# Separate weight tiles for Q, K and V, and two moves of gate/up blocks in a fused layer-norm, sliding-window attention and gated-MLP kernel

## The chip, the cores and the metric

The kernel runs on one core of one Trainium2 chip. The metric is device time in microseconds (us), lower is better. TensorE (PE in the profile) does the matrix products, VectorE (DVE) and ScalarE (ACT) read the sums and do elementwise work, GpSimd (POOL) masks, and SyncE (SP) issues nearly all DMA transfers.

## The reference

```python
def reference(A_x, A_wqkv, A_wo, B_x, B_w_gate, B_w_up, B_w_down):   # S=2048, D=640, F=1536
    x = A_x
    xn = _layernorm(x, axis=-1)
    return x + _A_ref(xn, A_wqkv, A_wo) + _B_ref(xn, B_w_gate, B_w_up, B_w_down)

# _A_ref: H = 32 heads of 20, window of 256 positions
    q, k, v = (x @ wqkv) split into three and into heads
    scores = einsum("bhqd,bhkd->bhqk", q, k) * (Dh ** -0.5)
    mask = (idx[:, None] - idx[None, :] >= 0) & (idx[:, None] - idx[None, :] < W)
    p = softmax(where(mask, scores, -1e9))
    return einsum("bhqk,bhkd->bhqd", p, v) joined over heads @ wo

# _B_ref
    h = sigmoid(x @ w_gate) * (x @ w_up)
    return h @ w_down
```

All arrays are bf16. Attention and the gated MLP read the same normalised x; their results and x are added.

## The kernel before

The 2048 positions are worked in four chunks of 512. For each chunk the kernel normalises x, turns it (`xnT`, by DMA transposes for chunks 1 to 3), and then has three kinds of TensorE work beside attention itself. **Q/K blocks** (`proj_block`): ten a chunk, Q0 to Q4 and K0 to K4, each of five matmuls of 512 columns. The sums are copied to a staging tile `st` (VectorE for Q, ScalarE for K), stored to a DRAM scratch (`sq`, `sk`), and read back spread over partitions as `qT` and `kT` by `spread`. The pool of `st` has six buffers. **V blocks** (`g_v`): eight a chunk. **GLU blocks** (`g_gu`): twelve a chunk; each has five matmuls for the gate, a tanh on ScalarE, five matmuls for up, and one VectorE instruction that writes `h`. An **output stage** (`g_out`) adds, for the four rows of 128 positions of a chunk, `h` times `w_down` (`down`) and the attention result times `wo` (`add_wo`); its arguments `between` and `ahead` take GLU blocks that are worked between the first row's two kinds of sums, or ahead of them.

Attention of a chunk is a series of score steps (16 for chunk 0, 20 for the others, numbered through as t = 0 to 75). A step's scores (L490) go to one PSUM tile `ps`, of which there is one buffer; ScalarE takes the exponential (L496), GpSimd masks, and after the last step of a head group `pv` (L523) multiplies by V.

The order on every engine is the order of the program. Attention's steps are the skeleton; a planner (`Fill`) pulls the other work in between, in the order of the `fill.add` calls, each with a cost in nanoseconds for TensorE. A step pulls at least about 1800 ns of it, and more where work is left over. `fill.until("qk1")` at the start of chunk 1 takes all that is left of an entry. Entries of cost 0 only issue DMAs: x of the next chunk (`load_x`), `wo` turned in DRAM (`turn_wo`, eight transfers into `wo_i`), `w_down` (`load_wd`, five), and the zero pads of the second scratch (`clear_next`, two). In the list of before they stand between chunk 0's last GLU block and `qk1`. The helper `mix` alternates two generators. All of these transfers, the `st` stores, `load_wo` and the `spread` loads go through SyncE's queue in the order of the program:

```python
    fill.add("gu0b", mix(g_gu(0, 4, 12), norms1, 0), 8 * GU)
    fill.add("x2", later(load_x, 2), 0)
    fill.add("wo_i", later(turn_wo), 0)
    fill.add("wd", later(load_wd), 0)
    fill.add("pads", later(clear_next), 0)
    fill.add("qk1", g_qk(1), 50 * MM)
    fill.add("v1", mix(g_v(1), g_gu(1, 0, 2), 1, 2), 40 * 136 + 2 * GU)
```

The Q, K and V weights lie side by side in one SBUF tile `wqkv`. It is loaded by four transfers (V in two halves, Q, K). A Q/K block reads its weights with a stride of five elements.

Of the kernel before, what the change touches and what calls it, by code (L numbers as in the profile page):

```python
# [9 lines left out]
P = 128  # L10
S = 2048
D = 640
# [3 lines left out]
DC = D // P  # L16
# [9 lines left out]
HALF = 320  # L26
# [11 lines left out]
BF16 = mybir.dt.bfloat16  # L38
# [55 lines left out]
def kernel(  # L94
# [11 lines left out]
    nc = tc.nc  # L106
# [4 lines left out]
    def pool(name, bufs, **kw):  # L111
        return ctx.enter_context(tc.tile_pool(name=name, bufs=bufs, **kw))

    const = pool("const", 1)
# [22 lines left out]
    def load_x(c):  # L137
        t = xp.tile([P, SBC, D], BF16, name="xc")
        xc[c] = t
        nc.sync.dma_start(out=t, in_=xr[:, c * SBC:(c + 1) * SBC, :])  # L140

    wqkv = const.tile([P, DC, 3 * D], BF16, name="wqkv")
    wqkv_r = A_wqkv.rearrange("(c p) n -> p c n", p=P)
    wg = [const.tile([P, DC, FS], BF16, name=f"wg{k}") for k in range(F // FS)]
    wu = [const.tile([P, DC, FS], BF16, name=f"wu{k}") for k in range(F // FS)]
# [2 lines left out]

    ones = nc.const_aps.tensor(1.0, [P, CW], BF16)
    def load_wqkv(part):  # L150
        nc.sync.dma_start(out=wqkv[:, :, part * D:(part + 1) * D],
                          in_=wqkv_r[:, :, part * D:(part + 1) * D])

    xc[0] = xp.tile([P, SBC, D], BF16, name="xc")

# [1 line left out]
        queue.dma_start(out=xc[0][:, s, :], in_=xr[:, s, :])  # L157

    def load_v(hf):
        a = 2 * D + hf * HALF  # L160
        nc.sync.dma_start(out=wqkv[:, :, a:a + HALF], in_=wqkv_r[:, :, a:a + HALF])

    load_rows(0, nc.sync)
    load_rows(1, nc.sync)
    load_rows(3, nc.sync)
    load_v(0)
    load_rows(2, nc.sync)
    load_v(1)
# [12 lines left out]
    def load_gu(t, w, k, lo=0, hi=FS):  # L181
        nc.sync.dma_start(out=t[k][:, :, lo:hi],
                          in_=w.rearrange("(c p) f -> p c f", p=P)[:, :, k * FS + lo:k * FS + hi])
# [32 lines left out]
    def load_wo():  # L216
        for i in range(HG):
            nc.sync.dma_start(out=wo[32 * i:32 * i + 32, :, :],
                              in_=wo_i[i].rearrange("(m j) n -> j m n", j=32))
# [63 lines left out]
    def turn_block(c, s):  # L283
        nc.sync.dma_start(out=xnT[c][:, :, s * P:(s + 1) * P], in_=xns.pop((c, s)), transpose=True)
# [5 lines left out]
    qk = {}  # L290
    vt = {}

    def proj_block(w, c, m):


        base = 0 if w == "q" else D
        ps = ps_d.tile([P, CW], FP32, name="pqk", tag="d")
        for d in range(DC):
            wt = wqkv[:, d, base:base + D].rearrange("p (k m) -> p m k", m=DC)
            nc.tensor.matmul(ps, lhsT=wt[:, m, :], rhs=xnT[c][:, d, :],  # L300
                             start=(d == 0), stop=(d == DC - 1))
        st = stp.tile([P, CW], BF16, name="st")
        if w == "q":
            nc.vector.tensor_copy(out=st, in_=ps)
        else:
            nc.scalar.copy(out=st, in_=ps)
        dst = scratch[w, c % 2].rearrange("(h j) s -> h j s", j=32)
        nc.sync.dma_start(out=dst[:, 4 * m:4 * m + 4, :], in_=st)

    def spread(w, c, g0, g1):  # L310

        half, first = divmod(g0, GH)
        if first == 0:
            qk[w, c, half] = (qp if w == "q" else kp).tile([P, GH, CW], BF16, name=w + "T")
        src = scratch[w, c % 2].rearrange("(a b p) s -> b p a s", a=2, p=P)
        for b in range(g0 // 2, g1 // 2):
            o = 2 * b - half * GH
            nc.sync.dma_start(out=qk[w, c, half][:, o:o + 2, :], in_=src[b])

    def new_v(c, s):  # L320
        v = vp.tile([P, 2, VH], BF16, name="v")
        vt[c * SBC + s] = v
        nc.gpsimd.memset(v[:, :, 0:16 * VW].rearrange("p k (h d) -> p k h d", d=VW)[:, :, :, DH:VW], 0.5)
        nc.gpsimd.memset(v[:, :, 16 * VW:], 0.0)

    def project_v(c, s, hf, home=ps_d, tag="d"):
        ps = home.tile([P, CW], FP32, name="pv", tag=tag)
        for d in range(DC):
            nc.tensor.matmul(ps[:, 0:HALF], lhsT=xnT[c][:, d, s * P:(s + 1) * P],  # L329
                             rhs=wqkv[:, d, 2 * D + hf * HALF:2 * D + (hf + 1) * HALF],  # L330
                             start=(d == 0), stop=(d == DC - 1))
        return ps

# [7 lines left out]
    def proj_v(c, s, hf, copy):  # L341
        copy_v(c, s, hf, project_v(c, s, hf), copy)
# [21 lines left out]
    def g_turns(c):  # L364
        for s in range(SBC):
            turn_block(c, s)
            yield 0

    def g_qk(c):
        for w in "qk":  # L370
            for m in range(DC):
                proj_block(w, c, m)
                if c == 0 and w == "q" and m == 1:
                    load_x(1)
                if c == 0 and w == "q" and m == 3:
                    load_gu(wu, B_w_up, 0, FS // 2)
                if c == 1 and w == "q" and m == 3:
                    load_wo()
                if c and w == "k" and m == 1:
                    spread("q", c, 0, GH)  # L380
                yield 5 * MM
        if c == 0:
            spread("q", c, 0, 2)
            spread("k", c, 0, 2)
            spread("q", c, 2, 4)
            spread("k", c, 2, 4)

    def g_v(c):
        for s in range(SBC):
            new_v(c, s)  # L390
            for hf in range(2):
                proj_v(c, s, hf, nc.scalar.copy if hf else nc.vector.tensor_copy)
                if hf == 0:
                    yield 5 * 136
            if s == 0:
                spread("k", c, 0, 2)
                spread("k", c, 2, GH)
            if s == 1:
                spread("q", c, GH, NG)
                spread("k", c, GH, NG)  # L400
            yield 5 * 136
# [4 lines left out]
    def part(w, d, f):  # L406
        k, first = divmod(f * P, FS)
        return w[k][:, d, first:first + P]

    def g_gu(c, f0, f1):  # L410
        for f in range(f0, f1):
            pg = ps_d.tile([P, CW], FP32, name="pg", tag="d")
            for d in range(DC):
                nc.tensor.matmul(pg, lhsT=part(wg, d, f), rhs=xnT[c][:, d, :],  # L414
                                 start=(d == 0), stop=(d == DC - 1))
            th = tp.tile([P, CW], FP32, name="th")
            nc.scalar.activation(out=th, in_=pg, func=TANH, scale=0.5)  # L417
            yield 5 * MM
            pu = ps_d.tile([P, CW], FP32, name="pu", tag="d")
            for d in range(DC):  # L420
                nc.tensor.matmul(pu, lhsT=part(wu, d, f), rhs=xnT[c][:, d, :],  # L421
                                 start=(d == 0), stop=(d == DC - 1))
            h = hp.tile([P, CW], BF16, name="h")
            ht[c, f] = h
            nc.vector.scalar_tensor_tensor(out=h, in0=th, scalar=1.0, in1=pu, op0=ADD, op1=MULT)  # L425
            yield 5 * MM
# [39 lines left out]
    def g_out(c, between, ahead=()):  # L466
        nxt = new_rows(c, 0)
        for s in range(SBC):
            rows = nxt
            if s == 0:  # L470
                yield from ahead
            if s + 1 < SBC:
                nxt = new_rows(c, s + 1)
            ys = [ps_d.tile([P, CW], FP32, name=f"y{i}", tag="d") for i in range(2)]
            for y, cut in zip(ys, HALVES):
                yield from down(c, s, y, cut)
            if s == 0:
                yield from between
            outp(c, s, ys, rows)
            yield 10 * 136  # L480
# [117 lines left out]
    def mix(a, b, first, every=1, rest=True):  # L598

        for k, cost in enumerate(a):  # L600
            yield cost
            if k >= first and (k - first) % every == 0:
                yield next(b, 0)
        if rest:
            yield from b
# [74 lines left out]
    fill = Fill()  # L680
    GU = 10 * MM
    OUT = 4 * 34 * 136
    APART = 1800
    FIRST_PART = 1000
    def later(load, *args):
        load(*args)
        yield 0

    norms1 = g_norms(1, True)
    norms2 = g_norms(2, True)  # L690
    norms3 = g_norms(3, False)
    fill.add("gu0a", mix(g_gu(0, 0, 4), norms1, 4, 1, False), 4 * GU)
    fill.add("gu0b", mix(g_gu(0, 4, 12), norms1, 0), 8 * GU)
    fill.add("x2", later(load_x, 2), 0)
    fill.add("wo_i", later(turn_wo), 0)
    fill.add("wd", later(load_wd), 0)
    fill.add("pads", later(clear_next), 0)
    fill.add("qk1", g_qk(1), 50 * MM)
    fill.add("v1", mix(g_v(1), g_gu(1, 0, 2), 1, 2), 40 * 136 + 2 * GU)
    fill.add("out0", mix(g_out(0, g_gu(1, 2, 3)), norms2, 1, 1), OUT + GU)  # L700
    fill.add("x3", later(load_x, 3), 0)
    fill.add("qk2", g_qk(2), 50 * MM)
    fill.add("v2", mix(g_v(2), g_gu(1, 3, 7), 0, 1), 40 * 136 + 4 * GU)
    fill.add("gu1b", mix(g_gu(1, 7, 12), norms3, 0, 1, False), 5 * GU)
    fill.add("out1", mix(g_out(1, g_gu(2, 0, 1)), itertools.chain(norms3, g_turns(3)), 1, 3), OUT + GU)
    fill.add("qk3", g_qk(3), 50 * MM)
    fill.add("v3", mix(g_v(3), g_gu(2, 1, 5), 0, 1), 40 * 136 + 4 * GU)
    fill.add("gu2", g_gu(2, 5, 12), 7 * GU)
# [101 lines left out]
```

## Time and profile before

| what | us |
|---|---|
| time, median of 3 runs (lowest to highest) | 309.93 (309.67 to 310.23) |
| the profiled execution's own time | 309.64 |
| its span, first to last instruction | 307.9 |
| TensorE busy | 300.4 |
| ScalarE busy | 198.4 |
| VectorE busy | 171.2 |
| GpSimd busy | 168.7 |
| granted TensorE clock | 1.00 throughout |

The span is what the views divide; the 1.74 us between it and the execution's own time lie outside the first and last instruction. Times in the views count from the span's start. In a timeline line the columns are start, duration, engine, line of the kernel, operation, tile written and tiles read, shape and count; a bracket at the end tells how long the engine was idle before and what ended that. A waits line tells who waited for whom, the total in us, how often, and the longest. `PEld` is TensorE's weight load, `SPq` the issue of a DMA by SyncE, `ACTq` an instruction of ScalarE's sequencer. The ends of matmuls are modelled and overlap the next start.

### The profile page before, as it was taken

Reading aid. Unit: us, or ns where it says so; the run is one execution under the profiler, and the core shown is the slowest. Engines: PE = TensorE matmul, PEld = TensorE weight load, DVE = VectorE, ACT = ScalarE, POOL = GpSimd, SP = SyncE. Lnnn points to the kernel's source line nnn. Section 1 sums busy time; section 2 is a strip of 40 time slices with the busy share of each in tenths; the row PEclk is TensorE's granted clock in tenths of the full one; section 3 lists DMA queues with packets and bytes.
Section 4 is the critical chain, followed back from the end, with each engine's and each line's share of the span. In section 5 each row is a group of like instructions: output and inputs, shape, how many; then the busy total and the mean of one; then the engine's idle time right before and its main releaser. Section 6 shows DMA issues by size and latency. Waiting matters only on the chain.

```text
span 307.9 us, 9937 instructions
## 1 busy us (share of the span) xinstructions
PE 300.4 (98%) x4276; PEld 167.7 (54%) x4311; DVE 171.2 (56%) x339; ACT 198.4 (64%) x197; POOL 168.7 (55%) x308
## 2 busy tenths in 40 slices
PE   7999999999999999999999999999999999999995
PEld 3654444555657654554457654554546664444774
DVE  4633667648698364487946164383734536363523
ACT  6923877698854649888674547878585547688000
POOL 6000686687874828576672728457372937566000
PEclk9999999999999999999999999999999999999999
DMA  7997986984709363630015312650000200000202
GB/s 220 366 319 237 333 161 199 351 228 144 234 2 127 69 179 124 189 109 2 3 24 87 87 57 87 209 162 0 3 2 2 86 27 21 2 2 6 84 21 67
DMA packets 40460, 35.68 MB, mean 116 GB/s; under 512 B 10560, under 2 KB 39872, under 8 KB 40384
## 3 DMA queue, kind: packets, MB, share of 16 engines
q1 hardware_dynamic: 39552, 34.27, 38.6%
q10 hardware_dynamic: 864, 0.77, 0.8%
q8 instruction: 34, 0.56, 0.8%
q14 instruction: 10, 0.08, 0.1%
HBM read 23.63 MB, written 10.26 MB: 110 GB/s over the span
## 4 chain that ended last, share of the span: by engine, by line
PE 96%; issue 1%; DMA 1%; ACT 1%; DVE 0%; SPq 0%
PE y L435 18%; PE pu L421 17%; PE pg L414 17%; PE pqk L300 14%; PE ps L490 9%; PE pv L329 7%; PE y L442 7%; PE acc L523 6%; DMA xc<-in_A_x_dram 1%; PE pt L280 0%; ACT xn L620 0%; ACT xn L625 0%; DVE xn L631 0%; SPq L157 0%; ACT rstd L626 0%
## 5 line engine op out<-in xcount | busy, mean ns | idle before, releaser
L507 POOL TENSOR_SCALAR_AFFINE_SELECT pT<-pT 64x512 bf16<-64x512 bf16 (+1 forms) x256 | 157.1, 614 | 109.1 <-ACT pT L496 96.6
L496 ACT ACTIVATE pT<-ps 128x2048 bf16<-128x2048 f32 (+1 forms) x76 | 141.0, 1855 | 59.8 <-PE ps L490 57.9
L425 DVE SCALAR_TENSOR_TENSOR h<-th,pu 128x512 bf16<-128x512 f32 x48 | 32.8, 683 | 51.4 <-PE pu L421 44.9
L421 PE MATMUL pu<-xnT,wu 128*128 128x512 bf16 x228 | 59.0, 380 | 0.7 <-issue 0.2
L414 PE MATMUL pg<-xnT,wg 128*128 128x512 bf16 x226 | 58.5, 380 | 0.9 <-issue 0.3
L435 PE MATMUL y<-wd,h 128*128 128x320 bf16 (+2 forms) x396 | 56.8, 295 | 0.0
L300 PE MATMUL pqk<-xnT,wqkv 128*128 128x512 bf16 x191 | 45.4, 381 | 0.6 <-issue 0.2
L435 PEld LDWEIGHTS <-h 128*128 128x128 bf16 x396 | 36.7, 98 | 15.9 <-issue 1.8
L417 ACT ACTIVATE th<-pg 128x512 f32<-128x512 f32 x48 | 28.6, 595 | 15.5 <-PE pg L414 15.4
L414 PEld LDWEIGHTS <-wg 128*128 128x128 bf16 x240 | 22.3, 98 | 25.8 <-issue 2.0
L421 PEld LDWEIGHTS <-wu 128*128 128x128 bf16 x240 | 22.0, 98 | 25.5 <-issue 2.0
L300 PEld LDWEIGHTS <-wqkv 128*128 128x128 bf16 x200 | 22.5, 119 | 18.7 <-issue 1.4
L535 DVE STREAM_TRANSPOSE t<-acc 128x512 f32<-128x512 f32 x32 | 21.1, 696 | 20.1 <-PE acc L523 20.1
L490 PE MATMUL ps<-qT,kT 20*64 20x320 bf16 (+4 forms) x1440 | 32.1, 260 | 0.0
L490 PEld LDWEIGHTS <-kT 20*64 20x64 bf16 x1440 | 15.4, 103 | 24.9 <-issue 21.8
L446 DVE SCALAR_TENSOR_TENSOR rows<-y,rows 128x320 bf16<-128x320 f32 x30 | 14.4, 488 | 25.9 <-PE y L442 25.7
L547 DVE TENSOR_TENSOR on<-t,rec 128x320 bf16<-128x320 f32 (+4 forms) x48 | 27.8, 579 | 1.1
L329 PE MATMUL pv<-wqkv,xnT 128*128 128x320 bf16 x160 | 25.8, 300 | 0.0
L442 PE MATMUL y<-wo,oc 128*128 128x320 bf16 (+2 forms) x165 | 24.2, 295 | 0.0
L338 DVE CAST v<-pv 64x320 bf16<-64x320 f32 x29 | 14.1, 486 | 12.5 <-PE pv L329 12.3
L523 PE MATMUL acc<-pT,v 64*32 64x320 bf16 (+4 forms) x1440 | 19.7, 253 | 0.0
L523 PEld LDWEIGHTS <-v 64*32 64x32 bf16 x1440 | 16.2, 91 | 5.8 <-ACT pT L496 1.7
(48 smaller groups left out, 157.3 us busy)
## 6 DMA issues: line engine op xcount, KB each, us to landing
qT<-sq SPq DMA_DIRECT2D x16, 256.0 KB
kT<-sk SPq DMA_DIRECT2D x16, 256.0 KB
sq<-st SPq DMA_DIRECT2D x20, 128.0 KB
sk<-st SPq DMA_DIRECT2D x20, 128.0 KB
out_dram<-rows SPq DMA_DIRECT2D x15, 160.0 KB
wg<-in_B_w_gate_dram SPq DMA_DIRECT2D x4, 480.0 KB
wu<-in_B_w_up_dram SPq DMA_DIRECT2D x4, 480.0 KB
xc<-in_A_x_dram SPq DMA_DIRECT2D x3, 640.0 KB
```

The source lines that it names most:

```text
L300: nc.tensor.matmul(ps, lhsT=wt[:, m, :], rhs=xnT[c][:, d, :], start=(d == 0), stop=(d == DC - 1))
L329: nc.tensor.matmul(ps[:, 0:HALF], lhsT=xnT[c][:, d, s * P:(s + 1) * P], rhs=wqkv[:, d, 2 * D + hf * HALF:2 * D + (hf + 1) * HALF], start=( ...
L414: nc.tensor.matmul(pg, lhsT=part(wg, d, f), rhs=xnT[c][:, d, :], start=(d == 0), stop=(d == DC - 1))
L417: nc.scalar.activation(out=th, in_=pg, func=TANH, scale=0.5)
L421: nc.tensor.matmul(pu, lhsT=part(wu, d, f), rhs=xnT[c][:, d, :], start=(d == 0), stop=(d == DC - 1))
L425: nc.vector.scalar_tensor_tensor(out=h, in0=th, scalar=1.0, in1=pu, op0=ADD, op1=MULT)
L435: nc.tensor.matmul(y[:, 0:cut[1] - cut[0]], lhsT=ht[c, f][:, s * P:(s + 1) * P], rhs=wd[:, f, cut[0]:cut[1]], start=(f == 0), stop=False)
L442: nc.tensor.matmul(y[:, 0:cut[1] - cut[0]], lhsT=oc[c, m][:, s * P:(s + 1) * P], rhs=wo[:, m, cut[0]:cut[1]], start=False, stop=(m == DC - 1))
L490: nc.tensor.matmul(ps[a * U:(a + 1) * U, i, col * U:(col + n) * U], lhsT=qk["k", kc, o // GH][32 * i:32 * i + DH, o % GH + a, kb * U:(kb + ...
L496: nc.scalar.activation(out=pt[:, :, 0:width], in_=ps[:, :, 0:width], func=EXP, scale=SCALE)
L507: nc.gpsimd.affine_select(out=view, in_=view, pattern=[[0, HG], [0, n], [sign, U]], compare_op=GE, fill=0.0, base=base, channel_multiplier ...
L523: nc.tensor.matmul(acc[32 * i:32 * i + 32, q * U:(q + n) * U], lhsT=vt[kb][a * U:(a + 1) * U, u, h * VW:h * VW + 32], rhs=pt[a * U:(a + 1) ...
```

## The change

`wqkv` becomes a list of three tiles, one each for Q, K and V. GLU blocks 10 and 11 of chunk 0 leave the entry `gu0b` and become an entry `gu0c` behind `qk1`, so that the four DMA entries and the Q/K blocks of chunk 1 come two GLU blocks sooner in the program. In output stage 1 the GLU block (2, 0) goes from `between` to `ahead`, as output stage 2 has it already.

```diff
-    wqkv = const.tile([P, DC, 3 * D], BF16, name="wqkv")
+    wqkv = [const.tile([P, DC, D], BF16, name="w" + part) for part in "qkv"]
...
-        nc.sync.dma_start(out=wqkv[:, :, part * D:(part + 1) * D],
-                          in_=wqkv_r[:, :, part * D:(part + 1) * D])
+        nc.sync.dma_start(out=wqkv[part], in_=wqkv_r[:, :, part * D:(part + 1) * D])
...
-        a = 2 * D + hf * HALF
-        nc.sync.dma_start(out=wqkv[:, :, a:a + HALF], in_=wqkv_r[:, :, a:a + HALF])
+        a = hf * HALF
+        nc.sync.dma_start(out=wqkv[2][:, :, a:a + HALF], in_=wqkv_r[:, :, 2 * D + a:2 * D + a + HALF])
...
-        base = 0 if w == "q" else D
...
-            wt = wqkv[:, d, base:base + D].rearrange("p (k m) -> p m k", m=DC)
+            wt = wqkv["qk".index(w)][:, d, :].rearrange("p (k m) -> p m k", m=DC)
...
-                             rhs=wqkv[:, d, 2 * D + hf * HALF:2 * D + (hf + 1) * HALF],
+                             rhs=wqkv[2][:, d, hf * HALF:(hf + 1) * HALF],
...
-    fill.add("gu0b", mix(g_gu(0, 4, 12), norms1, 0), 8 * GU)
+    fill.add("gu0b", mix(g_gu(0, 4, 10), norms1, 0), 6 * GU)
...
     fill.add("qk1", g_qk(1), 50 * MM)
+    fill.add("gu0c", g_gu(0, 10, 12), 2 * GU)
...
-    fill.add("out1", mix(g_out(1, g_gu(2, 0, 1)), itertools.chain(norms3, g_turns(3)), 1, 3), OUT + GU)
+    fill.add("out1", mix(g_out(1, (), g_gu(2, 0, 1)), itertools.chain(norms3, g_turns(3)), 1, 3), OUT + GU)
```

## The prediction

> **What bounds the kernel now.** I read the page first, then the timelines of TensorE, ScalarE and SyncE around the moved work, then the waits at the second output stage.
>
> ```profile
> PE 300.4 (98%) x4276; PEld 167.7 (54%) x4311; DVE 171.2 (56%) x339; ACT 198.4 (64%) x197; POOL 168.7 (55%) x308
> ...
> PE 96%; issue 1%; DMA 1%; ACT 1%; DVE 0%; SPq 0%
> ```
>
> TensorE is busy for 98% of the span and carries 96% of the chain that ended last. Because ends of matmuls are modelled, I also took start-to-start distances from the trace. From 13 us on, a 512-column matmul takes 216 ns and a 320-column one 133 ns; each change from fill work to scores costs 96 ns more, always; every larger distance but one is a missing record. So TensorE has almost no idle time to give back, and any wait put in front of it is paid in full. The one real hole is at 154.93:
>
> ```profile
> PEld L435 <- DVE h L425: 0.4, 1, 0.4
> ```
>
> That is the waits view for 153 to 156 us. The down sums of output stage 1 reach block 11 of chunk 1, whose `h` VectorE ends at 155.09 (start 154.42, 0.67 us); the matmul due at 154.93 starts at 155.14. Cost: 0.21 us.
>
> The next three fences are the TensorE, ScalarE and SyncE timelines (start, duration, engine, line). TensorE, with score steps 9, 10 and 11 on L490 and Q/K blocks between:
>
> ```profile
> 58.14 0.43 PE L490 MATMUL ps<-qT,kT 20*64 20x320 bf16 x24
> 58.50 2.35 PE L300 MATMUL pqk<-xnT,wqkv 128*128 128x512 bf16 x9
> 60.78 0.37 PE L490 MATMUL ps<-qT,kT 20*64 20x320 bf16 x16
> 61.08 2.35 PE L300 MATMUL pqk<-xnT,wqkv 128*128 128x512 bf16 x10
> 63.37 0.42 PE L490 MATMUL ps<-qT,kT 20*64 20x320 bf16 x16
> ```
>
> ```profile
> 58.74 1.88 ACT L496 ACTIVATE pT<-ps 128x2048 bf16<-128x2048 f32 x1 [1.78 <-PE ps L490]
> 61.32 1.45 ACT L496 ACTIVATE pT<-ps 128x1536 bf16<-128x1536 f32 x1 [0.70 <-PE ps L490]
> 63.47 0.59 ACT L306 CAST st<-pqk 128x512 bf16<-128x512 f32 x1 [0.70 <-PE pqk L300]
> 63.96 1.88 ACT L496 ACTIVATE pT<-ps 128x2048 bf16<-128x2048 f32 x1
> 65.73 1.08 ACT L306 CAST st<-pqk 128x512 bf16<-128x512 f32 x2
> ```
>
> ```profile
> 44.94 0.71 SPq L140 DMA_DIRECT2D xc<-in_A_x_dram  x1
> 45.70 5.36 SPq L213 DMA_DIRECT2D wo_i<-in_A_wo_dram  x8
> 51.11 4.04 SPq L206 DMA_DIRECT2D wd<-in_B_w_down_dram  x5
> 55.52 0.60 SPq L179 DMA_DIRECT2D sq<-kT  x1
> 56.47 0.56 SPq L179 DMA_DIRECT2D sk<-kT  x1
> 57.56 5.28 SPq L308 DMA_DIRECT2D sq<-st  x4
> ```
>
> The last fence is the one that decides. Sixteen transfers (x of chunk 2, turned wo, wd, pads) stand on SyncE ahead of the first Q store of chunk 1 and keep it until 57. The Q/K staging pool `st` has six buffers; chunk 1 makes ten copies (Q0 to Q4 on VectorE, K0 to K4 on ScalarE). So the copy of K1, the seventh, needs the store of Q0 landed, K2 that of Q1, and so on. ScalarE's own semaphore instructions on L306 (view of that line, 64.6 to 65.2 us) show this wait already:
>
> ```profile
> L306 ACTq EVENT_SEMAPHORE  x4: 17/28/38, 64.7 to 65.1; - x4
> ```
>
> The trace's semaphore records have Q0's store landed at 64.70, Q1's at 65.05, Q2's at 65.39, Q3's at 65.85. ScalarE passes the wait for Q0 at 64.72 and for Q1 at 65.07. Before, this is hidden: the exponential of step 11 is running until 65.84 and K1's sums end only about then.
>
> **The change, part by part.**
>
> *Weights in three tiles.* Same bytes, same order, same 640- and 1280-byte rows; no instruction added. What goes is a false wait: the second Q weight load waits for the K weights, since a strided read is held against every transfer into the shared tile that its range overlaps. The K weights landed at 12.83; that load was due at 13.20, and the matmuls run at 216 ns from there. Saving 0; with loads a microsecond late it would be 0.6, and a loss I exclude, since no wait is added.
>
> *Two GLU blocks behind the K sums.* A GLU block is 10 x 216 = 2160 ns, a Q/K block 1080 ns, and the planner hands out 2160 a step here. So steps 6 to 12 keep their lengths; the ten Q/K blocks slide forward by exactly two steps (Q0 from 54.89 to 49.66, 5.23 us), and blocks 10 and 11 fill steps 11 and 12. TensorE's work is unchanged: 0. Q0 needs the turned chunk 1, whose last transpose landed at 47.10, 2.6 us ahead: 0. The sixteen transfers are called earlier in the program but stay behind the transposes and ahead of the stores on SyncE. SyncE was not waiting for sums: x went out at 44.94 as soon as the last transpose was issued, and from there each issue waits for the eighth DMA before it (semaphores go round eight). Q0's copy ended at 56.89 but its store waited for the last `wo_i` (57.41); Q1's for the first `wd` (landed 58.65). So an earlier Q0 cannot leave earlier, and its store still lands at 64.70.
>
> Now K1's sums end at 59.6 instead of 64.8. ScalarE takes its work in order: exponential 9 (58.74 to 60.62), copies K1 and K2, exponential 10, K3, K4, exponential 11. It stands at K1 until 64.72. Behind it is exponential 10, whose scores are ready at 61.2, and behind that scores 11: the scores tile `ps` has one buffer. Step by step: K1 starts at 64.8; from the row at 65.73 two copies and then the exponential at 66.67 are 0.94 us apart, so exponential 10 starts at 65.74 and, at 1.45 us, ends at 67.19; scores 11 start at 67.3, not 63.37. TensorE finishes K3 and K4 at 63.3 and has nothing else in its order: 3.9 us lost. Next, K3 and K4 copy until 68.1, exponential 11 ends at 69.85, and scores 12 are due at 67.3 + 2.64 = 69.94: no second wait. Blocks 10 and 11 lie behind the stall and cannot cover it. The bound on the other side: a chunk 3 Q store took 2.1 us to land (180.78 to 182.84); with that, Q0 would land at 59.6 and nothing waits. I take 64.70, because the queue in front of it is the same.
>
> *GLU block ahead of output stage 1.* Same sums; `h` of block 11 gets 2.2 us more, so the 0.21 us hole closes. The first wo sums of the stage stay in step 40, so attention results are no later. Small regroupings follow in steps 62 to 64 and 69 to 70, with the same number of changes to scores: 0.
>
> Sum: 3.9 - 0.2 = +3.7 us. On the profiled execution: 309.64 + 3.7 = 313.3, a span of 311.6. The median lies 0.29 above that execution, so 313.6.
>
> **The rivals.**
>
> *The stall also slows the clock, 315.9.* The ten warm-up matmuls at the start take 4.43 us, 443 ns each, against 216 later: TensorE ran at half rate for its first 4.4 us or more, though the granted clock reads 1.00. If the half rate returns after an idle stretch of 4 us, 4.4 to 5 us at half rate cost another 2.2 to 2.5. Against it: the profile has no idle stretch this long after the start. 0.14.
>
> ```profile
> 0.84 4.43 PE L233 MATMUL pwarm<-const-bfloat16-1.0 128*128 128x512 bf16 x10 [0.84 <-PEq L794]
> ```
>
> The Trainium skill, "TensorE: Matmul & The Clock Gate", section "HAM oscillation — how this bites in real kernels", says that an idle gap over about 3.4 us puts the array back to half rate. By that rule this rival would be the likelier one, though its window runs free, so an estimate from that page is that a 4.0 us gap holds a whole window in (4.0 - 3.4) / 3.4, about one case in six. No run here shows it yet.
>
> *No stall, 309.7.* If the first Q stores land four microseconds sooner than recorded, K1 does not wait and only the 0.2 us remains. For it: a free queue lands a store in 2.1 us. Against it: eight landings in a row, 57.41 to 64.70, are spaced by the transfers themselves. 0.10.
>
> *Faster, 308.9.* The first K load of chunk 1 lands at 77.94, and scores 16 read it at 78.26. If executions without the profiler run over that 0.32 us margin, before pays there and the earlier K sums save it, with the stores landing in time too. It decides once the load is over 1.1 us later than in the profile, which would make 0.8 us besides the 0.2. Against it: the chain to this load runs through the same late stores, not through the sums. 0.06.
>
> **How the numbers follow.** The plain stall has the remaining 0.70, hence 313.6. One microsecond more or less in the landing gives 312.6 to 314.6, a little beyond for latencies of issue; the slow-clock case reaches 316.1. So 312.3 to 316.1, which leaves out the two cases without a stall, 0.16. A difference of 0.2% (0.6 us) is about what a measurement of this kernel can tell from none. Slower: 0.70 + 0.14 = 0.84; within: 0.10; faster: 0.06.
>
> **What would show it.** Right: TensorE idle for about 3.9 us ahead of scores 11 near 63.4, with the wait put to ScalarE; K1's cast starting near 64.8, right after a Q0 store landing near 64.7 and issued near 57.5; no wait of TensorE for `h` in output stage 1; matmuls of 216 ns after the stall. Slow clock: 427 to 443 ns there. Wrong: K1's cast near 60.6, or a Q0 store leaving well before 57.

## The result and the profile after

The changed kernel takes 315.06 us (median of 6 runs, 314.73 to 316.09) against 310.08 us (6 runs, 309.42 to 310.68): ratio 1.0168, 95% interval 1.0147 to 1.019. It is 4.98 us slower. The profiled execution of the changed kernel was the slowest of the six, 316.09 us with a span of 314.3; why it stands 1 us above the median is told below. Line numbers of the changed kernel are 3 lower than before's from `proj_block` on (L487 is the scores, L493 the exponential, L303 and L301 the two copies to `st`).

The page of the changed kernel, busy time, granted clock by fortieths of the span, and the chain that ended last:

```profile
PE 302.0 (96%) x4276; PEld 168.2 (54%) x4311; DVE 170.1 (54%) x339; ACT 198.4 (63%) x197; POOL 168.8 (54%) x308
...
PEclk9999999978999999999999999999999999999999
...
PE 88%; DMA 7%; issue 1%; SPq 1%; DVE 1%; ACT 1%; ACTq 0%; DVEq 0%
```

The work is the same (4276 matmuls recorded), but transfers now make up 7% of the chain and the clock dips in two slices, 63 to 79 us. TensorE's timeline there:

```profile
60.87 2.35 PE L297 MATMUL pqk<-xnT,wk 128*128 128x512 bf16 x10
67.41 0.65 PE L487 MATMUL ps<-qT,kT 20*64 20x320 bf16 x16 [4.18 <-ACT pT L493]
68.39 1.91 PE L411 MATMUL pg<-xnT,wg 128*128 128x512 bf16 x4 [0.33 <-issue]
70.10 2.34 PE L418 MATMUL pu<-xnT,wu 128*128 128x512 bf16 x5
72.37 0.65 PE L487 MATMUL ps<-qT,kT 20*64 20x320 bf16 x16
72.95 1.25 PE L411 MATMUL pg<-xnT,wg 128*128 128x512 bf16 x5
```

K3 and K4 end at 63.2; scores 11 start at 67.41 after 4.18 us of idleness that ScalarE's exponential ended. Then five matmuls take 2.34 us instead of 1.24: half rate. ScalarE in the same stretch:

```profile
58.56 1.88 ACT L493 ACTIVATE pT<-ps 128x2048 bf16<-128x2048 f32 x1 [0.90 <-PE ps L487]
64.93 1.07 ACT L303 CAST st<-pqk 128x512 bf16<-128x512 f32 x2 [4.49 <-DMA sq<-st]
65.89 1.47 ACT L493 ACTIVATE pT<-ps 128x1536 bf16<-128x1536 f32 x1
67.23 1.10 ACT L303 CAST st<-pqk 128x512 bf16<-128x512 f32 x2
68.21 1.90 ACT L493 ACTIVATE pT<-ps 128x2048 bf16<-128x2048 f32 x1
```

Exponential 9 ends at 60.44, and the copies of K1 and K2 start 4.49 us later, released by the landing of a Q store. Exponential 10 is behind them, and scores 11 start 0.05 us after it ends at 67.36. SyncE shows why that store is late:

```profile
45.45 5.27 SPq L212 DMA_DIRECT2D wo_i<-in_A_wo_dram  x8
50.95 4.46 SPq L205 DMA_DIRECT2D wd<-in_B_w_down_dram  x5
...
58.11 3.37 SPq L305 DMA_DIRECT2D sq<-st  x4
```

The first store leaves at 58.11 (57.56 before) although its sums are 5 us earlier; the semaphore records have it landed at 64.77 (64.70 before). The changed kernel's time windows, cut at the clock's own records (window and length, busy time of PE, PEld, DVE, ACT and POOL with instructions, then granted clock, DMA share and GB/s):

```profile
62.00:66.07 4.07, 1.23 (x6) 0.56 (x5) 0.00 (x0) 1.14 (x3) 0.96 (x3) 1.00 0.86 250
66.07:72.89 6.82, 5.15 (x41) 1.70 (x41) 0.35 (x1) 4.63 (x5) 4.48 (x8) 0.50 0.65 206
72.89:78.00 5.11, 5.11 (x125) 3.08 (x118) 2.75 (x6) 3.56 (x3) 2.24 (x4) 1.00 0.64 189
```

The clock stands at 0.50 for 6.83 us, of which 5.48 lie after the stall. From scores 11 to the gate sums behind scores 12 it takes 5.54 us (67.41 to 72.95). With the full clock the same work takes 2.98 us, in the run with the later `wo_i` below (63.32 to 66.30). So the slow clock cost this execution 2.6 us.

### The profile page after: what moved, and what is told of

Same layout as the page of the kernel before. It is cut to its first block, busy times and chain, and to the rows that moved or that the text cites. A ratio compares the mean times of both kernels' runs of the same rounds, so it can differ in the third digit from the quotient of the medians.

```text
span 314.3 us, 9938 instructions
## 1 busy us (share of the span) xinstructions
PE 302.0 (96%) x4276; PEld 168.2 (54%) x4311; DVE 170.1 (54%) x339; ACT 198.4 (63%) x197; POOL 168.8 (54%) x308
## 4 chain that ended last, share of the span: by engine, by line
PE 88%; DMA 7%; issue 1%; SPq 1%; DVE 1%; ACT 1%; ACTq 0%; DVEq 0%
PE y L432 17%; PE pu L418 16%; PE pg L411 16%; PE pqk L297 10%; PE ps L487 8%; PE pv L326 7%; PE y L439 7%; PE acc L520 5%; DMA wd<-in_B_w_down_dram 3%; DMA wo_i<-in_A_wo_dram 2%; DMA sq<-st 1%; DMA xc<-in_A_x_dram 1%; ACT pT L493 0%; SPq L212 0%; PE pt L279 0%
## 5 line engine op out<-in xcount | busy, mean ns | idle before, releaser
L493 ACT ACTIVATE pT<-ps 128x2048 bf16<-128x2048 f32 (+1 forms) x76 | 141.0, 1855 | 62.5 <-PE ps L487 60.2
L418 PE MATMUL pu<-xnT,wu 128*128 128x512 bf16 x228 | 60.2, 386 | 0.7 <-issue 0.2
L411 PE MATMUL pg<-xnT,wg 128*128 128x512 bf16 x226 | 59.4, 385 | 1.2 <-issue 0.7
L487 PE MATMUL ps<-qT,kT 20*64 20x320 bf16 (+4 forms) x1440 | 32.6, 263 | 4.2 <-ACT pT L493 4.2
L487 PEld LDWEIGHTS <-kT 20*64 20x64 bf16 x1440 | 15.6, 104 | 29.4 <-issue 26.3
L544 DVE TENSOR_TENSOR on<-t,rec 128x320 bf16<-128x320 f32 (+4 forms) x48 | 26.7, 557 | 1.1
L326 PE MATMUL pv<-wv,xnT 128*128 128x320 bf16 x160 | 25.8, 300 | 0.0
L297 PE MATMUL pqk<-xnT,wk 128*128 128x512 bf16 x97 | 23.1, 382 | 0.2
L297 PE MATMUL pqk<-xnT,wq 128*128 128x512 bf16 x94 | 22.5, 381 | 0.6 <-issue 0.4
```

The lines of the kernel that those rows point to most:

```text
L487: nc.tensor.matmul(ps[a * U:(a + 1) * U, i, col * U:(col + n) * U], lhsT=qk["k", kc, o // GH][32 * i:32 * i + DH, o % GH + a, kb * U:(kb + ...
L493: nc.scalar.activation(out=pt[:, :, 0:width], in_=ps[:, :, 0:width], func=EXP, scale=SCALE)
```

## The experiments

Before's median in the comparisons is 310.0 to 310.2 us; each ratio is against it, with its 95% interval.

**The GLU move alone.** Edit of before:

```diff
-    fill.add("gu0b", mix(g_gu(0, 4, 12), norms1, 0), 8 * GU)
+    fill.add("gu0b", mix(g_gu(0, 4, 10), norms1, 0), 6 * GU)
...
     fill.add("qk1", g_qk(1), 50 * MM)
+    fill.add("gu0c", g_gu(0, 10, 12), 2 * GU)
```

> The kernel before with the second part alone (GLU blocks 10 and 11 of chunk 0 behind the Q/K blocks of chunk 1). Staging theory: the whole loss is here, TensorE idle 4 to 4.4 us ahead of scores 11 and matmuls of 427 ns for 3 to 5 us after it; 315.0 to 315.5, since only the 0.2 us of the output stage is missing. Rival, that the three tiles or the output-stage move share in the loss: 312 to 314.

Measured 315.80 us, ratio 1.0193 (1.0167 to 1.0219). The whole loss is here, and 0.7 us more than with the other parts. TensorE's timeline has the same stall, 4.02 us long, and the clock is 0.50 from 66.97 to 70.38:

```profile
67.31 0.65 PE L490 MATMUL ps<-qT,kT 20*64 20x320 bf16 x16 [4.02 <-ACT pT L496]
```

The time is 0.3 us over the expected range. The waits of output stage 1 (159 to 163 us) show a longer hole there than before's:

```profile
PEld L435 <- DVE h L425: 1.1, 1, 1.1
PE y L435 <- DVE h L425: 0.8, 1, 0.8
```

VectorE ends `h` of block 11 at 161.13; the down matmul that needs it is 0.92 us late (start-to-start 1052 ns against 133), where before's was 0.21.

**The `wo_i` transfers behind the Q/K blocks.** Edit of the changed kernel:

```diff
-    fill.add("wo_i", later(turn_wo), 0)
...
     fill.add("qk1", g_qk(1), 50 * MM)
+    fill.add("wo_i", later(turn_wo), 0)
     fill.add("gu0c", g_gu(0, 10, 12), 2 * GU)
...
+    fill.add("wo", later(load_wo), 0)
     fill.add("out0", ...)
# and in g_qk:
-                if c == 1 and w == "q" and m == 3:
-                    load_wo()
```

> The changed kernel with the eight wo_i transfers issued behind the Q/K blocks of chunk 1 instead of ahead of them, and wo loaded ahead of output stage 0. Staging theory: without the eight transfers in front, Q0's store leaves near 51.5 and lands by 56, K1's cast starts near 60.4, no stall, no slow clock: 309.6 to 310.2. Rival, that ten Q/K blocks in a row at this place overload ScalarE or VectorE by themselves: the stall stays, 313 to 315.

Measured 309.22 us, ratio 0.9976 (0.996 to 0.9993), a little below the expected range. ScalarE's timeline, then the row of SyncE's with the stores of Q0 to Q4:

```profile
58.72 1.88 ACT L491 ACTIVATE pT<-ps 128x2048 bf16<-128x2048 f32 x1 [0.91 <-PE ps L485]
60.49 1.07 ACT L303 CAST st<-pqk 128x512 bf16<-128x512 f32 x2
61.44 1.48 ACT L491 ACTIVATE pT<-ps 128x1536 bf16<-128x1536 f32 x1
```

```profile
52.04 5.35 SPq L305 DMA_DIRECT2D sq<-st  x5
```

K1 is copied straight behind exponential 9, with the same ten Q/K blocks in a row; scores 11 start at 63.32. Q0's store leaves at 52.04 and lands at 58.62, later than the expected 56 but ahead of 60.5. So the row of Q/K blocks does not hurt by itself. It was what stood ahead of their stores. (The four `wo` loads moved too, but in the changed kernel they leave from 61.80 on, behind the stores of Q0 to Q3 for which K1 to K4 wait.)

**Eight `st` buffers.** Edit of the changed kernel: `pool("stp", 6)` becomes `pool("stp", 8)`.

> The changed kernel with eight st buffers instead of six. Staging theory: K1 and K2 copy at once, exponential 10 is on time, scores 11 run at 63.2; K3 and K4 wait for Q0 and Q1 until 64.8 and 65.1, exponential 11 ends near 67.6, scores 12 wait 1.7 us instead of 4.2; idle stretch too short for the slow clock, so matmuls stay at 216 ns: 311.4 to 311.9. Rival, that the stores' late issue delays chunk 1 in another way than through the buffers (spread loads, SyncE): as the changed kernel, near 315.

Measured 311.92 us, ratio 1.0058 (1.0027 to 1.009). Waits of that kernel:

```profile
ACT st L303 <- DMA sq<-st: 2.0, 1, 2.0
PE ps L487 <- ACT pT L493: 1.8, 1, 1.8
```

The time is at the upper edge of the expected range. The wait now comes at K3 and meets scores 12, 1.8 us long (1.7 was expected), with the clock at 1.00 there; of the six runs one, at 312.78, has 0.995. The stores leave as late as in the changed kernel (57.52, landed 64.74). Only the number of buffers differs, so it is the buffers that hand the lateness on.

**K4's sums three times over.** Edit of the changed kernel:

```diff
-        for d in range(DC):
+        for d in [*range(DC)] * (3 if (w, c, m) == ("k", 1, DC - 1) else 1):
```

> The changed kernel with K4's five matmuls of chunk 1 done three times over (each time from a fresh start, the same sums): ten more matmuls, 2.16 us, inside the stall. Theory that the idle stretch slows the clock: TensorE idles 2 us instead of 4.2, the stall ends at the same time, matmuls after it stay at 216 ns, 313.3 to 313.9, which is 1 to 2 us faster than the changed kernel although it does more work. Rival, that the slow stretch has another cause than idleness: 315.0 again; rival, that TensorE's work is the bound there: 317.

Measured 313.93 us, ratio 1.0123 (1.0096 to 1.0151): 1.1 us faster than the changed kernel with ten matmuls more, and each of its four runs (312.97 to 314.45) is faster than any of the changed kernel's.

```profile
60.91 4.51 PE L297 MATMUL pqk<-xnT,wk 128*128 128x512 bf16 x20
67.10 0.42 PE L487 MATMUL ps<-qT,kT 20*64 20x320 bf16 x16 [1.67 <-ACT pT L493]
67.68 1.03 PE L411 MATMUL pg<-xnT,wg 128*128 128x512 bf16 x4 [0.16 <-issue]
68.54 1.24 PE L418 MATMUL pu<-xnT,wu 128*128 128x512 bf16 x5
```

The stall ends at nearly the same place (67.10 against 67.41), but after 1.67 us of idleness, and the matmuls after it run at full rate. This separates the two prices, as differences of medians: the wait, less what the output stage gains, 313.93 - 310.07 = 3.9 us; the slow clock, the 1.1 us more.

**K4's sums twice.** The same edit with 2 for 3.

> The changed kernel with K4's five matmuls of chunk 1 done twice instead of three times: 1.08 us more work inside the stall, an idle stretch of about 3.0 us instead of 4.2 (changed kernel) or 1.7 (three times). If the clock falls only after an idle stretch of some 3.4 us, no run slows and the time is that of the version with three times, 313.6 to 314.2 with clocks of 0.998 and over. If the price grows steadily with the idle time, some runs show 0.995 and less, and the median lies between that version and the changed kernel, 314.3 to 314.8.

Measured 314.97 us, ratio 1.0139 (1.0109 to 1.0169); clocks 0.994 or 0.995 in three runs, 1.0 in three, of which one took 313.0 and two took 315.1 and 315.4. The first expectation fell. The time is above the second one's range too, so a steadily growing price isn't shown either. Windows of the profiled execution:

```profile
64.71:68.12 3.41, 0.76 (x18) 0.36 (x18) 0.00 (x0) 3.24 (x5) 0.70 (x2) 1.00 0.91 265
68.12:71.53 3.41, 3.41 (x9) 1.06 (x7) 0.00 (x0) 2.43 (x3) 2.87 (x5) 0.50 0.36 108
```

TensorE idled 3.02 us and was already working again, 0.76 us, when the clock fell. What makes the two slow runs at full clock is not known. Before's own runs with a clock of 1.0 spread from 309.3 to 311.9, so the cause need not lie in the stall.

**The three tiles alone.** Edit of before: the three-tile lines of the diff, nothing else.

> The kernel before with the three weight tiles alone. Forecast's reading: the false wait of the second Q weight load was never the last one, so 0: 309.9 to 310.2, the first Q matmul at 13.0 to 13.2 as before. Rival, that loads are late in some runs and the wait binds there: up to 0.6 us faster, 309.4 to 309.8.

Measured 310.22 us, ratio 1.0002 (0.9986 to 1.0018). The false wait costs nothing that can be measured.

**The output stage alone.** Edit of before: the `out1` line of the diff.

> The kernel before with the GLU block ahead of output stage 1 alone. Reading of the waits: TensorE's hole before h of block 11 closes, 0.2 us by the first trace, up to 0.9 us where VectorE is later, as in the run with the GLU move alone: 309.2 to 309.9. Rival, that the hole only moves to the wo sums or to a PSUM buffer: 310.1.

Measured 309.33 us, ratio 0.9969 (0.9953 to 0.9985). TensorE's timeline:

```profile
153.22 1.25 PE L414 MATMUL pg<-xnT,wg 128*128 128x512 bf16 x5
154.31 1.24 PE L421 MATMUL pu<-xnT,wu 128*128 128x512 bf16 x5
155.48 0.42 PE L490 MATMUL ps<-qT,kT 20*64 20x320 bf16 x16
155.84 3.43 PE L435 MATMUL y<-wd,h 128*128 128x320 bf16 x24
```

The GLU block runs first, `h` of block 11 is ready at 154.88, and the 24 down matmuls follow without a hole. The median gain, 0.67 us, is over the 0.21 us of before's trace and below the 0.92 us of the GLU move's. The three other traces with the old stage (the three tiles alone above, and the next two experiments) have 0.21 to 0.22 us again, so the hole as traced does not account for the whole gain.

**The later `wo_i` alone.** Edit of before: the `wo_i` and `wo` lines of the second experiment, without the GLU move.

> The kernel before with only the wo_i transfers issued behind the Q/K blocks of chunk 1, and wo loaded ahead of output stage 0; GLU blocks where they were. Staging theory: nothing waits for a Q store, but the first K load of chunk 1 now stands behind eight issues on SyncE, lands 3 to 5 us later than 77.9, and scores 16 at 78.3 wait for it: 312 to 315. Rival, that this load has room to spare: 309.8 to 310.2.

Measured 316.09 us, ratio 1.019 (1.0157 to 1.0223).

```profile
PE ps L488 <- DMA kT<-sk: 3.6, 1, 3.6
```

Scores 16 wait for the first K load (landed 83.30 against 77.94 before). The profiled execution was also some 1.5 us late from its start on (first Q sums at 14.66 against 13.20), where its clock came up later than in the others. The median is above the expected range; five of the six runs have a clock of 0.987 to 0.995, so the clock fell in those as well. A transfer train that leaves one place must have room at the next.

**The GLU move with the later `wo_i`.** Both edits on before, without tiles and output stage.

> The GLU move and the later wo_i transfers together, without the three tiles and without the change of output stage 1. Staging theory: neither wait is left, only the hole at h of block 11 in output stage 1: 309.9 to 310.3, some 0.2 to 0.9 us over the version that has all parts (309.2). Rival, that the tiles or the output stage made that version's whole gain and the later transfers cost: over 310.5.

Measured 309.64 us, ratio 0.9999 (0.9975 to 1.0022), 0.4 us over the version with all parts and a little below the expected range. With the Q/K blocks two GLU blocks sooner, the first K load leaves SyncE at 70.62 (76.84 in the run before) and lands at 76.78, ahead of scores 16 at 78.15. So the later train has the room that it lacked; the pair gains nothing over before. What beats both kernels is the output stage, alone (309.33) or with all parts and the later `wo_i` (309.22); the two can't be told apart by their intervals.

## Why the prediction was right, and where it was off

The direction and the range (312.3 to 316.1) held; the time was 1.5 us over the forecast of 313.6. It is also above the 312.6 to 314.6 that the plain stall was given. The range held because its upper end came from the slow-clock rival, so that it held is in part luck.

*The stall.* Its steps came out one by one: Q0's store landed at 64.77 (forecast 64.70), K1's copy started at 64.93 (64.8), exponential 10 ended at 67.36 (67.19), scores 11 started at 67.41 (67.3), scores 12 did not wait for the exponential. (The slow clock would have hidden a short wait. At full clock, with K4 three times over, scores 12 come 2.75 us after scores 11, 0.13 us more than in the run with the later `wo_i`, so there is next to none.) TensorE idled 4.18 us (3.9); the work ahead of the stall ran 0.21 us earlier in this execution (scores 9 at 57.93 against 58.14) and only waited longer. The GLU move alone shows the whole loss. The later `wo_i` and eight buffers each changed one link of this chain, and the time followed; K4 three times over left the stall's end where it was.

*The clock.* Here a step failed: the chance of 0.14 for the slow clock, which came to pass in every run of the changed kernel (granted 0.989 to 0.995 over the span) and of the GLU move alone (0.989 to 0.994). The forecast reasoned that the profile had no long idle stretch, which says nothing about what one does. The rival's price, 2.2 to 2.5 us, is near that of two slow periods of 3.41 us each, 2.6 us in the changed kernel's trace; two of its six runs have the clock of that trace, 0.989. The other four have 0.994 or 0.995, as the trace of K4 twice has with one period. One period cost 1.4 us in the GLU move's trace (4.41 us from scores 11 to the same gate sums, against 2.98), and the medians with and without it differ by 1.1. So for most runs the price was over-sized. The second period is why the profiled execution is the slowest.

The Trainium skill, "TensorE: Matmul & The Clock Gate", section "HAM oscillation — how this bites in real kernels", warns of idle gaps over about 3.4 us; the trace agrees that such a gap halves the rate (0.50 from 66.07 on). The estimate of one case in six, drawn from it by asking for a wholly idle window, did not hold: the clock fell in all ten runs of the changed kernel and of the GLU move alone, and in the trace of K4 twice a window with 0.76 us of work was enough. The length of the gap does not decide it either: there it was 3.02 us, while 3.55 us in the profiled execution of the later `wo_i` alone left the clock at 1.00. On this the measurement differs from the figure of the Trainium skill.

*The output stage.* Forecast -0.2; measured -0.67 us alone and -0.7 within the change (315.06 against 315.80, from two comparisons). The term was read from one execution, and its size is confirmed by three other traces (0.21 to 0.22 us); only the GLU move's trace has more, 0.92. That the hole is longer in many executions that left no trace would explain the median, but is not shown, so the rest of this gain stays open.

*The tiles* came out as forecast, 0. The sum with the terms as measured: from scores 9 to scores 11 it takes 9.48 us instead of 5.23, so 4.25; with 1.1 for the clock and -0.67 for the output stage 4.7, with the trace's 1.4 for the clock 5.0. Measured were 4.98; as the terms come from different executions, so close a fit is partly chance.

The rivals without a stall and on the faster side did not come: the stores landed as recorded, and scores 16 waited for nothing in either kernel.

## What to carry to other kernels

When work is moved earlier, follow every buffer that it fills to the transfer that empties it: if that transfer stands in a queue whose place is set by other transfers, the work only reaches the wait sooner. On an engine that works in order, such a wait stops whatever is queued behind it, here the exponential that frees the only scores tile. Where TensorE is the bound, an idle stretch can cost more than its length: here stretches of 3.0 to 4.2 us added 1.4 to 2.6 us at half rate in three of the four traces that have one, and the stretches of 1.7 and 1.8 us added none in theirs.

## What the runs showed of the hardware

The clock's records lie on a grid of 3.413 us that runs through each execution (61.44, 6.83, 3.413 and 303.8 us are its multiples). The clock fell after grid periods in which TensorE worked 0.00 us (GLU move alone), about 0.6 us (changed kernel) and 0.76 us (K4 twice). It stayed up after 1.5 us (later `wo_i` alone, its profiled execution), 1.6 us (eight buffers) and 2.3 us (K4 three times). It fell at the period's end, with K4 twice 0.76 us after the stall was over, and came back one period later, or two in the changed kernel, where work filled only 1.74 us of the first (2.74 with the GLU move alone). So neither the length of the gap nor its end alone tells whether it is paid. The place of the grid differs from run to run: at the start, before's clock reaches full at 5.82 us and that of the later `wo_i` alone at 10.07 us, whose V sums until then take 267 ns a matmul instead of 136. Two of before's runs (311.21 and 311.49 us) have a clock of 0.994 too; what slowed it there, no trace shows.

The eight `wo_i` transfers move in packets of 25,600 bytes, four at a time and 0.95 us each. Behind them the parts of a transfer land unevenly: in the changed kernel twelve of the sixteen landing records of Q0's store come from 60.39 to 62.27, the last four from 64.11 to 64.77. With the `wo_i` transfers behind the Q/K blocks fifteen come by 57.18 and the last at 58.62. But from its issue to its last record the store takes as long there, 6.58 us against 6.66. Its 6.15 us of lateness go with the later issue, 58.11 against 52.04. How much the uneven landing would cost a store that was issued sooner is not shown.
